# A new hand-written order with batch 0's chain at its head, and output blocks stored as one transfer each, in a fused attention and token-mixing kernel

## The chip, the cores and the metric

The kernel runs on one core of a Trainium2 chip. Its time is the device time of one execution in microseconds (us), as a median over runs; beside that there is one profiled execution with its own time and a trace. Engines: PE is TensorE (PEld its weight loads), ACT is ScalarE, DVE is VectorE, POOL is GpSimd, SP is the sync engine, which here only issues transfers.

## What is computed

```python
def _attn_ref(q, k, v, p):              # q, k, v: (8, 8, 576, 64), p: (8, 8, 32, 64)
    scale = 1.0 / np.sqrt(q.shape[-1])
    def sm_attn(qq, kk, vv):
        s = scale * np.matmul(qq, kk.transpose(0, 1, 3, 2))
        a = np.exp(s - np.max(s, axis=-1, keepdims=True))
        return np.matmul(a / (np.sum(a, axis=-1, keepdims=True) + 1e-09), vv)
    p_packed = sm_attn(p, k, v)
    return sm_attn(q, p_packed, p_packed)

def _moe_ref(x, w_q, w_k, w_out):       # x: (8, 576, 512), w_q, w_k: (512, 64), w_out: (512, 512)
    wq, wk = x @ w_q, x @ w_k
    W_tok = np.einsum('bsd,btd->bst', wq, wk) / np.sqrt(w_q.shape[1])
    return np.maximum(np.einsum('bst,btd->bsd', W_tok, x), 0.0) @ w_out
```

The attention's output, with its 8 heads laid side by side, is the x of the second part. The output is (8, 576, 512) in float32.

## The kernel before

The work is cut into some 75 small operations per batch, each a Python function (`s0`, `pv`, `m0`, `o3` ...), for eight batches. Their order is written out by hand in the string `SCHEDULE`; a loop at the end of the kernel reads it from left to right and emits the instructions. Each engine works through its own part of the list strictly in order, so the list is at once the order on PE, ACT, DVE, POOL and SP.

An entry is `name@batch`, then what it needs: digits after a colon are the PSUM banks that a PE operation writes (five banks, 0 to 4, are dealt out this way; the other three hold the scores `s` and `e` in turn); a `c` or `f` after them says whether a 128-wide matmul is cut into two halves of 64 columns or left full; a trailing `s` or `v` is the engine that copies a result from PSUM to SBUF ("evicts" it), ACT or DVE; `g` is POOL (for `ml`), `p` and `s` behind `sc` are the queue that issues the store, SP or ACT.

The chain of one batch, in the names of the list:

- `LK`, `LQ`, `LV`: loads of k, q and v (576 KB each as bf16), issued by POOL, which also issues the loads of p and the weights (`LP`, `cw0` to `cw3`, `wo0`, `wo1`). Each goes to one of six buffers (`SLOTS`).
- `kt`, `ke` and `qt`, `qe`: k and q are transposed on PE in three parts and evicted. Batch 0 is different: its k comes in float32 by two SP transfers (`k_f`, line 171, halves A and B), is cast to bf16 (`cA0`, `cA1`, `cB0`, `cB1`), transposed (`kf0`, `kf1` from half A, `kf2`, `kf3` from half B) and evicted (`kfe0` to `kfe3`). `tp` and `lp` bring batch 0's p into the block matrix `pT_bd`, which `s` uses; `tr`, `lq0`, `lq1` bring that of the other batches.
- `s0`, `nm0` (or `nmA`, `nmB`), `ex0`, `ex1`, `rc1`: scores of p against k, their maximum (DVE), exponentials (ACT), reciprocals of the sums.
- `xt`, `xe`, `pv`, `pp`, `pt`, `pte`: the exponentials transposed and evicted, times v, scaled and masked, transposed.
- `e0`, `mx`, `sb`, `x`, `sm`, `rr`, `ml`: scores of q against the 32 packed rows, and their softmax (DVE for `mx`, `sb`, `sm`, `rr`, ACT for `x`, POOL or DVE for `ml`).
- `at`, `ae`, `pq`, `wk`, `wq`, `g`, `y`, `m0`, `m1`, `m2` with their evictions (`wke`, `wkx`, `wqe`, `ge`, `ye`, `r00` ... `r2`): the token mixing in a reordered form; `wq`, evicted by `wqe` to the tile `wqT`, holds one column per token.
- `o0` to `o4`, `oe0` to `oe4`: the projection with `w_out` in four blocks of 128 tokens and a fifth that two batches share, evicted to `o_sb0`, `o_sb1` (two blocks each) and `ox`.
- `st0`, `st1`, `st2` store `o_sb0`, `o_sb1`, `ox` from SP. For the last batch `sc0` to `sc3` store one block each, from SP or ACT.

The 576 tokens of a batch are laid out as 64 rows `sp` of 9 tokens `j`. Tokens of column group `j2` (0 or 1) lie in partitions 64\*j2 to 64\*j2+63 of `o_sb`, which is why each store is two transfers:

```python
for j2 in range(2):
    nc.sync.dma_start(ov[:, 4 * j2 + 2 * i:4 * j2 + 2 * i + 2, :], S_[b][f"o_sb{i}"][64 * j2:64 * j2 + 64])
```

`wm` at the head of the list runs matmuls on the identity whose result nobody reads (24 pairs of 64x128 with 128 columns).

Of the kernel before, what the change touches and what calls it, by code (L numbers as in the profile page):

```python
# [7 lines left out]


SCHEDULE = """  # L10
    wm@24:3 LQ@0 LV@0 LP@0 LK@1 LK@2 cB1@0s cA0@0s kf3@0:3 cw1@0 tp@0:1 kfe3@0s cw3@0 lp@0v
# [6 lines left out]
    pqe@0s xt1@1:1c qe0@1s ml0@0v xt0@1:3c at1@0:2c rc1@1 xe1@1v xe0@1s s0@2 qe1@1v at0@0:0c
    ae1@0s nm0@2 pv@1:43 ae0@0s LQ@3 ex1@2 wk@0:0c pp0@1 pp1@1 wq@0:1 wke@0s wkx@0 ex0@2
    pt@1:4c g@0:2 pte@1v wqe@0s rc1@2 e0@1:f ge@0v LK@5 y@0:3 xt0@2:0c mx0@1 ye@0s kt1@3:4  # L20
    xe0@2s pq@1:2 LQ@4 m0@0:31 pqe@1s xt1@2:0c r01@0s sb0@1 kt0@3:2 r00@0s LV@4 kt2@3:1
    ke0@3s o1@0:3c ke2@3v x0@1 ke1@3v m1@0:21 oe1@0v o0@0:4c r10@0s sm0@1 r11@0s qt2@2:2
    s0@3 xe1@2s oe0@0s qt1@2:1 rr0@1 nm0@3 o2@0:0c qe2@2s ml1@1g qt0@2:3 ml2@1g oe2@0v
    qe0@2s pv@2:24 ml0@1g qe1@2v ex0@3 at1@1:0c LK@6 pp1@2 at0@1:3c pp0@2 ae1@1s o3@0:1c
    LQ@5 ae0@1v ex1@3 pt@2:3c wk@1:0c pte@2s LK@7 wq@1:4 wke@1s wkx@1 rc1@3 pq@2:2 wqe@1s
    g@1:3 e0@2:f pqe@2s ge@1v oe3@0s y@1:4 xt0@3:0c mx0@2 ye@1s st1@0 m0@1:31 LQ@6 xt1@3:4c
    r01@1s kt1@4:2 xe1@3v st0@0 r00@1s kt0@4:1 xe0@3v ke1@4s sb0@2 pv@3:34 ke0@4s kt2@4:0
    pp0@3 x0@2 o1@1:2c LV@5 pp1@3 ke2@4v qt0@3:3 sm0@2 oe1@1s m2@1:0c s0@4 qe0@3s qt1@3:1
    r2@1s pt@3:2c rr0@2 o0@1:4c nm0@4 pte@3s ml2@2g ml0@2g qt2@3:3 oe0@1s o4@1:2c qe2@3v
    ex1@4 ml1@2g qe1@3v at0@2:3c kt2@5:0 ex0@4 ae0@2v kt0@5:1 LQ@7 at1@2:3c oe4@1s ke0@5v  # L30
    e0@3:c ke2@5s ae1@2v m1@1:12 mx0@3 wk@2:4c r11@1s xt0@4:3f r10@1s xt1@4:2f rc1@4 wke@2s
    wkx@2 pq@3:0 kt1@5:1 xe1@4s sb0@3 o3@1:4c pqe@3s ke1@5s qt1@4:0 oe3@1v xe0@4s s0@5
    qe1@4v x0@3 wq@2:2 nm0@5 g@2:1 qt2@4:4 ge@2s wqe@2s pv@4:13 sm0@3 ex0@5 ex1@5 o2@1:2c
    pp0@4 pp1@4 y@2:1 qt0@4:0 qe2@4v oe2@1s pt@4:3c qe0@4v ye@2s kt2@6:4 pte@4s rr0@3
    m0@2:12 ke2@6v m1@2:30 r01@2s ml1@3g e0@4:c r10@2v r00@2s xt0@5:2f rc1@5 r11@2s mx0@4
    ml2@3g kt0@6:4 ml0@3g xe0@5s pq@4:0 kt1@6:3 o3@2:1c pqe@4s ke1@6v ke0@6s LV@6 sb0@4
    at1@3:0c LV@7 o1@2:4c ae1@3s oe3@2v at0@3:3c x0@4 kt0@7:2 ae0@3v o0@2:0c ke0@7v oe1@2s
    sm0@4 kt1@7:2 oe0@2s kt2@7:4 s0@6 ke2@7s ke1@7v wq@3:3 qt2@5:2 wqe@3s qt0@6:4 qe2@5v
    qt1@5:0 qe0@6s wk@3:3c rr0@4 nm0@6 xt1@5:1f ml2@4g qe1@5s o2@2:2f ml0@4g xe1@5s wkx@3
    qt1@6:0 ex0@6 oe2@2v ml1@4g pv@5:41 wke@3v ex1@6 st1@2 qe1@6v g@3:2 pp1@5 at1@4:3f pp0@5  # L40
    ge@3s st1@1 at0@4:0f ae1@4s qt2@6:2 ae0@4v xt0@6:1c rc1@6 qe2@6s xt1@6:4c st0@1 xe0@6v
    s0@7 xe1@6v y@3:1 pt@5:3c nm0@7 ye@3s qt2@7:2 st0@2 pte@5s qt0@7:4 qe2@7s qt0@5:0
    wk@4:3c qe0@7v ex0@7 pv@6:21 wkx@4 qe0@5v wke@4s ex1@7 m1@3:34 pp0@6 qt1@7:0 r11@3s
    pp1@6 e0@5:c r10@3s qe1@7v m2@3:4f mx0@5 xt0@7:1f r2@3s xt1@7:0f o2@3:3f xe0@7s rc1@7
    xe1@7s sb0@5 o4@3:4f oe2@3s g@4:1 pt@6:3f ge@4v x0@5 wq@4:0 pte@6v pq@5:2 oe4@3v y@4:1
    o3@3:3c pqe@5s sm0@5 wqe@4s e0@6:c ye@4s oe3@3s m0@4:40 rr0@5 pv@7:21 st1@3 r01@4s mx0@6
    ml0@5g r00@4s m0@3:30 o1@4:4c r01@3s ml1@5g sb0@6 r00@3s o0@4:0c oe1@4s ml2@5g pp1@7
    x0@6 at1@5:4c pp0@7 at0@5:3c o1@3:1c ae1@5v oe0@4s sm0@6 o0@3:4c ae0@5s oe1@3s pq@6:3
    wk@5:2c oe0@3s rr0@6 pt@7:0f ml1@6g wke@5s wkx@5 st0@3 m1@4:41 pte@7s pqe@6v g@5:2
    r11@4s r10@4v e0@7:f ml2@6g ge@5s st2@1 ml0@6g pq@7:2 wq@5:4 mx0@7 pqe@7s at1@6:0c  # L50
    wqe@5s y@5:2 at0@6:3c o2@4:1c ae0@6s ae1@6v ye@5s sb0@7 wk@6:4c oe2@4s m0@5:02 wke@6s
    o3@4:3f r00@5s wkx@6 r01@5v x0@7 g@6:1 oe3@4v m1@5:04 o0@5:2c ge@6s sm0@7 r10@5s st1@4
# [17 lines left out]
def kernel(  # L70
# [60 lines left out]
    def halves(m):  # L131
        return (slice(0, P),) if m == "f" else (slice(0, 64), slice(64, P))

    def bank(k, shape, dtype, name):
        return psK.tile(shape, dtype, tag=f"k{k}", name=name)

    def evict(on, dst, src, func=COPY, scale=1.0):
        if on == "s":
            nc.scalar.activation(dst, src, func, scale=scale)  # L139
        elif func == RELU:  # L140
            nc.vector.tensor_scalar(dst, src, 0.0, None, op0=MAX)
        elif scale != 1.0:
            nc.vector.tensor_scalar(dst, src, scale, None, op0=MULT)
        else:
            nc.vector.tensor_copy(dst, src)  # L145
# [515 lines left out]

    def store_block(c, b, on):
        eng = nc.scalar if on == "s" else nc.sync
        ov = out[b].rearrange("(sp j) d -> sp j d", j=NJ)
        for j2 in range(2):
            eng.dma_start(ov[:, 4 * j2 + c, :], S_[b][f"o_sb{c // 2}"][64 * j2:64 * j2 + 64, c % 2])
# [62 lines left out]
```

## Time and profile before

| | |
|---|---|
| three runs | 132.22, 133.68, 132.2 us; median 132.22 us |
| the profiled execution | 131.66 us |
| its span, first to last instruction | 129.6 us |
| mean granted clock of PE | 0.934 of full speed |
| busy PE / DVE / ACT / POOL | 108.7 / 93.2 / 95.3 / 41.5 us |
| loads, issued by POOL | 14.49 MB, 66.7% of 16 DMA engines' span |
| stores and the first loads, issued by SP | 10.16 MB, 26.4% |

How to read the lines shown below: a group or a piece is named by engine, source line and `out<-in` with the program's tile names; x12 is a count; what stands in brackets is the engine's idle time just before and what ended it. In stretches (`a:b`) stand the elapsed time, the busy time of each engine with its instruction count, the granted clock, the DMA share and GB/s. Matmuls are pipelined, so busy times of neighbouring groups overlap a little.

### The profile page before, as it was taken

How to read it: one execution, taken by the hardware profiler on the slowest of the kernel's cores; microseconds unless marked ns; L12 is line 12 of the kernel's file. 1: busy time of each engine (PE TensorE's matmuls, PEld its weight loads, DVE VectorE, ACT ScalarE, POOL GpSimd, SP SyncE). 2: the span in 40 equal slices, each digit the busy share in tenths (PEclk: the TensorE clock that was granted, in tenths of full speed). 3: DMA queues.
4: the chain of work that ended last, by engine and by line, in shares of the span. 5: the costliest groups of instructions: out<-in, count | busy, mean ns of one | idle time of the engine just before them, and what ended most of it. 6: DMA issues, size and time to landing. Idle time of an engine off the chain costs nothing.

```text
span 129.6 us, 4472 instructions
## 1 busy us (share of the span) xinstructions
PE 108.7 (84%) x1940; PEld 78.7 (61%) x1944; DVE 93.2 (72%) x158; ACT 95.3 (74%) x187; POOL 41.5 (32%) x61
## 2 busy tenths in 40 slices
...
PEclk9995558967999999999999999999999999999995
...
GB/s 47 358 199 210 210 193 200 211 204 205 208 207 209 206 211 207 275 293 210 206 209 207 199 206 142 260 295 106 0 167 28 215 24 259 229 224 212 284 196 122
DMA packets 18275, 25.45 MB, mean 196 GB/s; under 512 B 2512, under 2 KB 14800, under 8 KB 18256
## 3 DMA queue, kind: packets, MB, share of 16 engines
q0 software_dynamic: 13920, 14.49, 66.7%
q1 hardware_dynamic: 4016, 10.16, 26.4%
q10 hardware_dynamic: 320, 0.52, 1.7%
...
## 4 chain that ended last, share of the span: by engine, by line
PE 49%; DVE 21%; ACT 16%; DMA 4%; issue 3%; ACTq 1%; SPq 1%; DVEq 0%
PE o_ps L640 15%; PE tp_h L272 8%; PE pv L347 4%; DVE nmax L303 4%; DVE mx L430 4%; DMA k_f<-in_k_dram 4%; DVE e L433 4%; PE s L294 3%; ACT e1T L312 3%; PE e_ps L413 3%; DVE rs L444 2%; ACT o_sb L139 2%; ACT kT L139 2%; PE m_ps L603 2%; ACT e L440 2%
## 5 line engine op out<-in xcount | busy, mean ns | idle before, releaser
L468 POOL TENSOR_TENSOR a<-e,rr 128x512 bf16<-128x512 f32 (+1 forms) x21 | 16.9, 828 | 52.7 <-DVE rr L447 27.8
L640 PE MATMUL o_ps<-w_out,reluT 128*64 128x512 bf16 (+1 forms) x216 | 31.7, 380 | 0.4 <-DVE wkx L543 0.2
L640 PEld LDWEIGHTS <-reluT 128*64 128x64 bf16 (+1 forms) x220 | 13.3, 108 | 10.2 <-issue 1.4
L139 ACT ACTIVATE reluT<-m_ps 128x512 bf16<-128x512 f32 x27 | 14.7, 601 | 1.7 <-PE m_ps L603 1.5
L139 ACT ACTIVATE o_sb<-o_ps 128x512 f32<-128x512 f32 (+1 forms) x24 | 13.6, 588 | 2.5 <-PE o_ps L640 2.3
L312 ACT ACTIVATE e1T<-s,nmax 128x576 bf16<-128x576 f32 x16 | 11.8, 740 | 4.5 <-DVE nmax L303 4.5
L272 PE MATMUL tp_h<-ident,q_sb 128*64 128x128 bf16 x288 | 13.1, 242 | 0.0
L272 PEld LDWEIGHTS <-q_sb 128*64 128x64 bf16 x288 | 11.5, 126 | 2.3 <-issue 0.9
L303 DVE TENSOR_REDUCE nmax<-s 128x2 f32<-128x1152 f32 (+1 forms) x9 | 10.7, 1200 | 2.9 <-PE s L294 2.9
L139 ACT ACTIVATE kT<-tp_h 128x768 bf16<-128x768 bf16 (+2 forms) x14 | 10.5, 780 | 2.3 <-PE tp_h L232 1.3
L430 DVE TENSOR_REDUCE mx<-e_ps 128x36 f32<-128x1152 f32 (+2 forms) x9 | 10.9, 1216 | 1.5 <-PE e_ps L402 1.0
L272 PE MATMUL tp_h<-ident,k_sb 128*64 128x128 bf16 x252 | 10.3, 224 | 1.1 <-ACT kT L139 0.9
L444 DVE TENSOR_REDUCE rs<-e 128x36 f32<-128x1152 f32 (+2 forms) x9 | 10.9, 1214 | 0.3 <-ACT e L440 0.2
L433 DVE TENSOR_TENSOR e<-e_ps,mx 128x1152 f32<-128x1152 f32 (+2 forms) x9 | 10.9, 1218 | 0.2
L347 PE MATMUL pv<-v_sb,e 64*128 64x256 bf16 x144 | 10.5, 287 | 0.2 <-DVE e L145 0.2
L440 ACT ACTIVATE e<-e 128x1152 f32<-128x1152 f32 (+2 forms) x9 | 9.6, 1067 | 0.9 <-DVE e L433 0.9
L272 PEld LDWEIGHTS <-k_sb 128*64 128x64 bf16 x252 | 8.6, 112 | 2.3 <-issue 1.5
L139 ACT ACTIVATE qT<-tp_h 128x768 bf16<-128x768 bf16 x11 | 8.7, 820 | 0.7 <-PE tp_h L272 0.7
L145 DVE COPY o_sb<-o_ps 128x512 f32<-128x512 f32 x9 | 6.1, 683 | 3.9 <-DMA out_dram<-o_sb 2.6
L355 DVE SCALAR_TENSOR_TENSOR pp<-pv,rrec,mask 128x256 bf16<-128x256 f32 x16 | 7.0, 479 | 2.4 <-PE pv L347 2.3
L294 PE MATMUL s<-kT,pT_bd 128*64 128x64 bf16 (+3 forms) x64 | 6.3, 322 | 2.8 <-ACT kT L139 2.8
L347 PEld LDWEIGHTS <-e 64*128 64x128 bf16 x144 | 7.1, 99 | 2.1 <-DVE e L145 0.6
...
## 6 DMA issues: line engine op xcount, KB each, us to landing
out_dram<-o_sb SPq DMA_DIRECT2D x28, 256.0 KB, 3.8
q_sb<-in_q_dram POOLq DMA_DIRECT2D x8, 576.0 KB, 17.5
v_sb<-in_v_dram POOLq DMA_DIRECT2D x8, 576.0 KB, 14.3
k_sb<-in_k_dram POOLq DMA_DIRECT2D x7, 576.0 KB, 15.3
k_f<-in_k_dram SPq DMA_DIRECT2D x2, 576.0 KB, 4.7
out_dram<-ox SPq DMA_DIRECT2D x8, 128.0 KB, 3.3
w_out<-in_moe_w_out_dram POOLq DMA_DIRECT2D x2, 256.0 KB, 11.4
out_dram<-o_sb ACTq DMA_DIRECT2D x4, 128.0 KB, 2.4
```

The lines of the kernel that those rows point to most:

```text
L139: nc.scalar.activation(dst, src, func, scale=scale)
L272: nc.tensor.transpose(tp[64 * g2:64 * g2 + 64, 2 * gp:2 * gp + 2, jj, :], S_[b][src][:, gp + 2 * g2, order[3 * t + jj]], ident,)
L294: nc.tensor.matmul(ps[64 * gp:64 * gp + 64, S * h2 + c0:S * h2 + c1], pT_bd[:, b, 2 * gp + h2].rearrange("d g l -> d (g l)"), S_[b]["kT"][ ...
L303: nc.vector.tensor_reduce(tile("nmax", [P, 2], fp32, b)[:, r], S_[b]["s1"][:, r], axis=AX, op=MAX, negate=True)
L312: nc.scalar.activation(tile("e1T", [P, NJ, 2, 64], bf16, b)[:, :, h2], S_[b]["s1"][:, h2].rearrange("r (j s) -> r j s", j=NJ), EXP, bias=S ...
L347: nc.tensor.matmul(ps[h2], S_[b]["e1"][r, j, :], S_[b]["v_sb"][r, :, j, :].rearrange("s (g gp) d -> s gp g d", gp=2), start=(j == 0), stop ...
L430: nc.vector.tensor_reduce(tile("mx", [P, NU, 1], fp32, b)[:, r], S_[b]["e"][:, r], axis=AX, op=MAX)
L433: nc.vector.tensor_tensor(tile("e2", [P, NU, L], fp32, b)[:, r], S_[b]["e"][:, r], S_[b]["mx"][:, r].to_broadcast((P, nu, L)), op=SUB,)
L440: nc.scalar.activation(e, e, EXP, scale=scale)
L444: nc.vector.tensor_reduce(tile("rs", [P, NU, 1], fp32, b)[:, r], src[:, r], axis=AX, op=ADD)
L468: (nc.gpsimd if on == "g" else nc.vector).tensor_tensor(tile("a2", [P, NU, L], bf16, b)[:, r], S_[b]["e2"][:, r], S_[b]["rr"][:, r].to_bro ...
L640: nc.tensor.matmul(ps[r], src[:, i, o:o + P][:, r], w_out[:, i, :], start=(i == 0), stop=(i == 3),)
```

## The change

The list is reordered from end to end (600 entries in both, the same operations but for `wm`): of the engine letters 43 evictions change from ACT to DVE and 35 from DVE to ACT, and `ml0` and `ml2` of batch 0 go from DVE to POOL. Batch 0's head now begins with `tp`, then a smaller `wm` (5 pairs, 512 columns each), then the casts and transposes of half A ahead of those of half B. In the last batch `sc2` is issued by ACT and `sc0`, `sc1`, `sc3` by SP; before, it was `sc0`, `sc3` by ACT and `sc1`, `sc2` by SP.

`wqe` writes the columns of `wqT` interleaved, so that partition 2\*sp + j2 of an output block holds what was in partition 64\*j2 + sp. The 128 partitions of a block then follow the order of the rows in the output, and `st0`, `st1` and each `sc` become one transfer from 128 partitions where there were two from 64. `st2` keeps its two.

```diff
@@ SCHEDULE
-    wm@24:3 LQ@0 LV@0 LP@0 LK@1 LK@2 cB1@0s cA0@0s kf3@0:3 cw1@0 tp@0:1 kfe3@0s cw3@0 lp@0v
-    cB0@0s cw0@0 cA1@0v kf2@0:4 kf1@0:0 kfe2@0v kf0@0:1 kfe0@0s kfe1@0s s0@0 nmA@0 nmB@0
-    ex0@0 qt0@0:2 LQ@1 qt2@0:0 ex1@0 qt1@0:1 qe0@0s xt0@0:3c xt1@0:4c xe0@0v qe2@0s xe1@0v
-    rc1@0 qe1@0s pv@0:34 cw2@0 pp1@0 tr@0:20 pp0@0 LV@1 pt@0:1c lq0@0v pte@0s lq1@0s e0@0:c
-    mxB@0 kt1@1:2 LK@3 kt0@1:0 mxA@0 kt2@1:4 sbB@0 ke2@1s sbA@0 xB@0 ke1@1s smB@0 kt2@2:4
-    wo1@0 kt1@2:1 ke0@1s rrB@0 wo0@0 ml1@0v ke2@2s s0@1 LQ@2 ke1@2v xA@0 nm0@1 LV@2 kt0@2:1
-    ke0@2v ex0@1 smA@0 qt2@1:2 LV@3 ex1@1 pq@0:3 qt0@1:0 ml2@0v rrA@0 qt1@1:4 qe2@1v LK@4
...
-    ae0@7s wk@7:4c st0@5 oe4@5v m0@6:01 wke@7s wkx@7 m1@6:23 r01@6s r00@6v g@7:4 st2@3
-    r11@6s wq@7:1 r10@6s o0@6:0c wqe@7v st2@5 ge@7s y@7:3 o1@6:2c ye@7s oe0@6s m1@7:13
-    m2@7:4f r11@7s o2@6:0f r2@7v oe1@6s r10@7v o3@6:3f oe2@6s st0@6 o4@7:2f oe3@6s st1@6
-    m0@7:30 oe4a@7v oe4b@7s o2@7:1f r00@7s r01@7s st2@7 o3@7:4f oe2b@7s oe2a@7s o1@7:0f
-    sc2@7p oe3@7s sc3@7s o0@7:3f oe1@7v sc1@7p oe0@7s sc0@7s
+    tp@0:0 wm@5:1 LQ@0 LV@0 cA0@0s cA1@0v LP@0 lp@0v LK@1 kf1@0:0 LK@2 cB0@0v cB1@0s kf0@0:4
+    kfe1@0s kf3@0:1 cw1@0 kfe0@0v kf2@0:2 kfe3@0s cw3@0 kfe2@0v s0@0 cw0@0 nmB@0 nmA@0
+    qt2@0:2 ex1@0 cw2@0 qt1@0:0 qt0@0:1 qe1@0v ex0@0 qe0@0v qe2@0s xt1@0:4c xt0@0:3c xe1@0s
+    xe0@0v rc1@0 pv@0:10 LQ@1 tr@0:32 pp0@0 LV@1 pp1@0 pt@0:0c lq0@0v pte@0s lq1@0s e0@0:c
+    mxB@0 kt2@1:4 LK@3 kt0@1:3 mxA@0 ke2@1s kt1@1:0 sbA@0 ke1@1s sbB@0 xA@0 ke0@1v xB@0
+    kt0@2:0 smA@0 wo1@0 kt2@2:3 s0@1 smB@0 wo0@0 ke2@2s kt1@2:4 LQ@2 rrA@0 rrB@0 pq@0:3
+    ke1@2s nm0@1 ml2@0g LV@2 ml1@0v ml0@0g ex0@1 ke0@2v at1@0:4c ex1@1 LK@4 qt0@1:2 ae1@0v
...
+    oe2@5v ml0@7g ye@6v m2@5:0c oe3@5s at1@7:2c r2@5v m0@6:31 ae1@7s st1@5 at0@7:4f r00@6v
+    o4@5:0f r01@6s st1@4 ae0@7v st0@5 m1@6:21 oe4@5v wq@7:3 r11@6s wk@7:4c st2@5 r10@6s
+    o0@6:0f wke@7s wkx@7 wqe@7s g@7:1 oe0@6s o1@6:4f ge@7s y@7:1 o3@6:3c ye@7v oe1@6v
+    m2@7:2c m1@7:10 r2@7s st0@6 o2@6:4f r10@7v r11@7s oe3@6s m0@7:20 oe2@6s o3@7:1f r00@7v
+    r01@7s st1@6 o4@7:2f oe3@7v o1@7:3f sc3@7p oe4a@7v oe4b@7s st2@7 o0@7:1f oe1@7s o2@7:3f
+    sc1@7p oe0@7s sc0@7p oe2a@7v oe2b@7s sc2@7s
...
@@ -558,7 +558,10 @@
 
     @op
     def wqe(b, on):
-        evict(on, tile("wqT", [P, 512], bf16, b), S_[b]["wq_ps"])
+
+
+        dst = tile("wqT", [P, 512], bf16, b).rearrange("r (c s j) -> r c j s", c=4, j=2)
+        evict(on, dst, S_[b]["wq_ps"].rearrange("r (c j s) -> r c j s", c=4, j=2))
 
     @op
     def g(b, ks):
@@ -647,23 +650,23 @@
         r = slice(0, D) if half is None else slice(D // 2 * half, D // 2 * half + D // 2)
         evict(on, dst[:, r], S_[b]["o", c][:, r])
 
+    def rows_of(b):
+        return out[b].rearrange("(sp r) d -> sp r d", r=NJ)[:, 0:8].rearrange("sp (j c) d -> sp j c d", c=4)
+
     def store(i, b):
         if i == 2:
             for e in range(2):
                 ov = out[b - 1 + e].rearrange("(sp j) d -> sp j d", j=NJ)
                 nc.sync.dma_start(ov[:, 8, :], S_[b]["ox"][64 * e:64 * e + 64])
             return
-        ov = out[b].rearrange("(sp j) d -> sp j d", j=NJ)
-        for j2 in range(2):
-            nc.sync.dma_start(
-                ov[:, 4 * j2 + 2 * i:4 * j2 + 2 * i + 2, :], S_[b][f"o_sb{i}"][64 * j2:64 * j2 + 64],
-            )
+        nc.sync.dma_start(
+            rows_of(b)[:, :, 2 * i:2 * i + 2].rearrange("sp j c d -> sp j (c d)"),
+            S_[b][f"o_sb{i}"].rearrange("p c d -> p (c d)"),
+        )
 
     def store_block(c, b, on):
         eng = nc.scalar if on == "s" else nc.sync
-        ov = out[b].rearrange("(sp j) d -> sp j d", j=NJ)
-        for j2 in range(2):
-            eng.dma_start(ov[:, 4 * j2 + c, :], S_[b][f"o_sb{c // 2}"][64 * j2:64 * j2 + 64, c % 2])
+        eng.dma_start(rows_of(b)[:, :, c], S_[b][f"o_sb{c // 2}"][:, c % 2])
 
     for c in range(4):
         ops[f"sc{c}"] = lambda b, on, c=c: store_block(c, b, on)
@@ -679,12 +682,11 @@
 
     @op
     def wm(n, ks):
-        ps = bank(ks[0], [P, 128], fp32, "warm")
+        ps = bank(ks[0], [P, 512], fp32, "warm")
+        moving = ident.unsqueeze(1).to_broadcast((P, 4, P))
         for _ in range(n):
-            for g2 in range(2):
-                nc.tensor.matmul(
-                    ps[64 * g2:64 * g2 + 64], ident[:, 64 * g2:64 * g2 + 64], ident, start=True, stop=True,
-                )
+            for r in halves("c"):
+                nc.tensor.matmul(ps[r], ident[:, r], moving, start=True, stop=True)
 
     for item in SCHEDULE.split():
         name, rest = item.split("@")
```

More of the change, by code (lines that the diff above doesn't have):

```diff
@@ L17 @@
-    ke0@2v ex0@1 smA@0 qt2@1:2 LV@3 ex1@1 pq@0:3 qt0@1:0 ml2@0v rrA@0 qt1@1:4 qe2@1v LK@4
[L18 to L52, printed above, removed]
@@ new lines @@
+    kt0@2:0 smA@0 wo1@0 kt2@2:3 s0@1 smB@0 wo0@0 ke2@2s kt1@2:4 LQ@2 rrA@0 rrB@0 pq@0:3
+    ke1@2s nm0@1 ml2@0g LV@2 ml1@0v ml0@0g ex0@1 ke0@2v at1@0:4c ex1@1 LK@4 qt0@1:2 ae1@0v
+    qt1@1:0 pqe@0s rc1@1 at0@0:1c LV@3 qe0@1v qe1@1s xt0@1:4c xt1@1:3c ae0@0v s0@2 xe1@1v
+    xe0@1v qt2@1:0 wk@0:3c nm0@2 qe2@1s pv@1:14 LQ@3 wke@0s wkx@0 ex0@2 wq@0:0 pp0@1 pp1@1
+    ex1@2 g@0:2 pt@1:1f ge@0v wqe@0v y@0:3 pte@1s xt0@2:4c ye@0s e0@1:c xe0@2s LK@5 pq@1:2
+    mx0@1 m0@0:30 pqe@1s m1@0:41 r00@0s r01@0s kt1@3:3 sb0@1 r10@0s o1@0:0c r11@0s kt2@3:2
@@ new lines @@
+    ke1@3v x0@1 o0@0:1c oe1@0v kt0@3:3 ke2@3s sm0@1 xt1@2:0c qt1@2:4 ke0@3s o2@0:2c oe0@0s
+    rr0@1 xe1@2v qt0@2:3 oe2@0s ml0@1g qe1@2v s0@3 qe0@2v qt2@2:4 ml1@1g nm0@3 at0@1:3c
+    qe2@2s pv@2:10 ml2@1g ae0@1v LQ@4 ex1@3 at1@1:2c rc1@2 pp0@2 o3@0:4c LV@4 ae1@1s pp1@2
+    pt@2:3c LK@6 ex0@3 wq@1:2 pte@2v wk@1:1c LQ@5 wqe@1s xt1@3:3f xt0@3:0f wke@1s xe1@3v
+    e0@2:f xe0@3s wkx@1 rc1@3 kt0@4:1 oe3@0s mx0@2 kt1@4:2 ke0@4s g@1:0 st1@0 pq@2:4 kt2@4:3
+    ge@1s st0@0 ke1@4v pqe@2s y@1:1 sb0@2 ye@1s m0@1:41 pv@3:02 r00@1s ke2@4v x0@2 m2@1:4c
```

28 lines of the change are left out of this document (26 added, 2 removed).

## The prediction

> **What bounds the kernel now.** I read the page's busy table and its slices first. All times are microseconds unless marked ns; a slice is 3.24 us, its digit the clock granted to TensorE in tenths.
>
> ```profile
> span 129.6 us, 4472 instructions
> PE 108.7 (84%) x1940; PEld 78.7 (61%) x1944; DVE 93.2 (72%) x158; ACT 95.3 (74%) x187; POOL 41.5 (32%) x61
> ...
> PEclk9995558967999999999999999999999999999995
> ```
>
> TensorE is busiest, but its clock is at half in much of the first 32 us, so I looked at the kernel by stretches (elapsed time, then busy time of PE, PEld, DVE, ACT, POOL, then the clock).
>
> ```profile
> 30.50:122.62 92.12, 89.36 (x1603) 62.79 (x1602) 77.17 (x126) 79.52 (x159) 25.07 (x32) 1.00 0.92 196
> 122.62:129.60 6.98, 0.00 (x0) 0.00 (x0) 0.00 (x0) 0.60 (x1) 0.00 (x0) 0.75 0.63 172
> ```
>
> From 30.5 on TensorE is dense: 2.76 of 92.12 idle. Behind its last matmul stand 6.98 without it. So three things can move the end: when the dense middle starts, how much idle time the new order leaves in it, and the 6.98. The chain of waits (start, length, what) shows the first.
>
> ```profile
> 1.24 0.46 SPq L171
> 1.74 5.19 DMA k_f<-in_k_dram
> 6.95 1.26 ACT k_sb L139 x2
> 8.21 0.48 ACT kT L139
> 8.69 0.63 ACT k_sb L139
> 9.37 1.18 PE tp_h L232 x28
> 10.57 1.20 ACT kT L139 x2
> 11.81 1.19 PE s L294 x7
> 13.02 1.43 DVE nmax L303 x2
> 14.55 1.56 ACT e1T L312 x4
> 16.15 0.76 PE tp_x L330 x8
> 16.93 0.50 DVE e L145
> 17.48 2.43 PE pv L347 x18
> ```
>
> Nothing is computed for batch 0 until the second half of its k has landed at 6.93 (1.74 + 5.19); then casts, transposes, scores (`s`), softmax and `pv` follow in line. The timeline shows the end.
>
> ```profile
> 121.66 1.18 ACTq L666 DMA_DIRECT2D out_dram<-o_sb  x2
> 121.79 0.69 DVE L145 COPY o_sb<-o_ps 128x512 f32<-128x512 f32 x1 [2.60 <-DMA out_dram<-o_sb]
> 122.94 0.60 ACT L139 ACTIVATE o_sb<-o_ps 128x512 f32<-128x512 f32 x1 [1.31 <-PE o_ps L640]
> 123.57 1.12 ACTq L666 DMA_DIRECT2D out_dram<-o_sb  x2
> 124.25 2.65 SPq L666 DMA_DIRECT2D out_dram<-o_sb  x4
> ```
>
> The last block is in SBUF at 123.54, but SP begins four of the last eight half stores only at 124.25 and needs 2.65 to issue them.
>
> **Part 1, the front.** Before, the first casts are `cB1` and `cA0`, both on ACT: the half of k that lands first waits for the other. After, `cA0` (ACT) runs beside `cA1` and `lp` (DVE), and TensorE's order is `kf1 kf0 kf3 kf2`.
>
> ```profile
> k_f<-in_k_dram SPq DMA_DIRECT2D x1, 576.0 KB, 4.2
> L145 DVE CAST k_sb<-k_f x1: 516/516/516, 9.1 to 9.1; 128x512 bf16<-128x512 f32 x1
> L143 DVE TENSOR_SCALAR pT_bd<-tp_p x2: 283/288/294, 8.4 to 8.7; 64x128 bf16<-64x128 f32 x2
> 12.73 2.18 PE L272 MATMUL tp_h<-ident,q_sb 128*64 128x128 bf16 x36
> ```
>
> The first of the two k_f issues takes 4.2 to landing (last column), so half A is there at 1.24 + 4.2 = 5.45. `cA1` (0.52) ends at 5.97, the two instructions of `lp` (0.29 each) at 6.5. `kf1` writes the bank that `lp` reads, so it starts at 6.55. A transpose takes 2.18/36 = 61 ns at half clock (the last row lies in a half-clock slice), 1.18/28 = 42 ns at a mostly full one. At half clock, argued below, `kf1` (8 of them) and `kf0` (10) end at 7.65. Half B lands at 6.93, its casts (ACT 0.63, DVE about 0.65) end at 7.6, so `kf3` and `kf2` end at 8.73. `kfe1` and `kfe3` on ACT (1.20 for two) end at 8.8; `kfe2` on DVE (0.5) at 9.3. `s` starts at 9.35 instead of 11.81, 2.46 earlier. From there I use the chain's durations: `s` to 10.55, `nmax` to 12.0, the exponentials to 13.65. Then 0.4 is given back, because `xt1` now stands ahead of `xt0`, whose copy `pv` needs first: 18 transposes at about 65 ns to 14.85, `xe0` 0.50, `pv` at 15.45 instead of 17.48. The steps behind `pv` keep their order. **Front: -2.0.**
>
> The moved pieces around it: `qe1` and `qe0` go from ACT to DVE (about 0.55 each, by the 0.50 of the chain's `DVE e` for a sixth less) and run in DVE's gap between `nmax` (12.0) and `xe0` (14.85); without that gap they would cost 1.1. `tp` now stands ahead of the warm-up and waits for p_f, which SP issues before k_f and which is a ninth of half A in size; TensorE's next work for the chain is `kf1` at 6.55, so this costs nothing. On ACT `qe2` stands ahead of `xe1`; both end by 15.1, before `pv`.
>
> The clock: the new warm-up has ten matmuls of 512 columns for forty-eight of 128.
>
> ```profile
> 106.85 1.73 PE o_ps L640 x16
> 6.60:10.00 3.40, 1.30 (x31) 1.02 (x33) 1.21 (x4) 2.37 (x4) 2.74 (x6) 1.00 1.18 202
> 13.40:16.80 3.40, 2.47 (x44) 2.04 (x40) 1.05 (x2) 2.25 (x6) 0.80 (x2) 0.50 1.22 210
> 16.80:20.25 3.45, 3.29 (x35) 2.09 (x33) 1.22 (x4) 1.40 (x3) 0.74 (x1) 0.50 1.42 195
> ```
>
> Two 64-wide matmuls of 512 columns run as a pair in 1.73/8 = 0.22, so the new warm-up lasts about 1.1, and the stretch before 6.6 holds about 1.4 busy of 3.4. After a stretch with 1.30 busy the clock went to half, after 2.47 it stayed there, after 3.29 it came back. So I take half clock from 6.6 (0.4 on the start of `s`, counted above) until `pv` has run. The new front has 2.8 busy in the 3.4 after 6.6, between 2.47 and 3.29: if that brings the clock back, `pv` takes 1.1 and `s` about half, and the front is -4; if the clock comes back one stretch later than before, about 1 is lost. I keep -2.0, range -1 to -4.
>
> [...]
>
> The loads: POOL's ninth load waits for its first to land, the tenth for the second, and so on, so the rows in which POOL waited date the landings of q, v and batch 1's k.
>
> ```profile
> 9.98 0.75 POOL L149 DMA_DIRECT2D q_sb<-in_q_dram  x1 [0.66 <-DMA q_sb<-in_q_dram]
> 12.84 0.61 POOL L253 DMA_DIRECT2D wqk<-in_moe_w_k_dram  x1 [2.11 <-DMA v_sb<-in_v_dram]
> 18.31 0.74 POOL L149 DMA_DIRECT2D k_sb<-in_k_dram  x1 [3.50 <-DMA k_sb<-in_k_dram]
> ```
>
> q is there by 9.98 and needed at 10.55, v by 12.84 and needed at 15.45, batch 1's k by 18.31 and needed about 20.5. `cw2` passes `LQ@1` on POOL, so `LQ@1` is issued at 12.84 instead of 9.98, still behind batch 1's k in a queue that is never empty (the DMA share, last column but one of the stretches, is 1.18 and more): no change. Two more `ml` of batch 0 move to POOL, ahead of `LV@2` and `LK@4`. They delay these issues by a few us; the eight loads in flight cover that, and without the cover `pv@2` would wait as long.
>
> **Part 2, the middle.** The matmul work is the same. Counted in the two lists, 43 evictions go from ACT to DVE and 35 the other way.
>
> ```profile
> L141 DVE TENSOR_SCALAR reluT<-m_ps 128x512 bf16<-128x512 f32 x5 | 3.4, 683 | 0.0
> L143 DVE TENSOR_SCALAR pT_bd<-tp_r x4: 375/381/395, 20.7 to 21.7; 64x224 bf16<-64x224 bf16 x4
> ```
>
> Net eight at about 0.66 put 5.3 on DVE and bring it to 98, still below TensorE. What the reshuffle does to the 2.76 of idle time can't be read from the trace; it can gain at most that. I take 0, with -1.5 to +2. The wqT eviction now writes its columns interleaved. The nearest copy that writes in scattered pieces is `lq`, 224 elements in 381 ns against 128 in 288 in `lp`: 1 ns for each further element, no dearer than a plain copy. So 0, and 0.7 at most (a doubled write on the last batch's path).
>
> [...]
>
> **Part 3, the end.** Each store becomes one transfer from 128 partitions; the last eight half stores become four.
>
> ```profile
> SPq L666 <- DMA out_dram<-o_sb: 2.6, 1, 2.6
> out_dram<-o_sb SPq DMA_DIRECT2D x4, 128.0 KB, 2.5
> out_dram<-o_sb SPq DMA_DIRECT2D x1, 256.0 KB, 3.0
> ```
>
> SP's wait of 2.6 is for another store. In the program the transfers of SP and ACT share eight completion counters in turn, and the one that `sc2` needs is held by `sc3`, which ACT issued at 121.66. With one transfer per store the last eight reach back to `st0@6`, and the wait goes. Late next is the last block itself: at TensorE's end T, two DVE half copies (0.85 for both, a whole one being 0.69), the issue at T+0.9 taking 0.56, and then what followed the last issue before, 129.6 - 126.9 = 2.7, plus 0.5 for 256 KB against 128 KB (3.0 against 2.5): T+4.7, and T+5.0 with the store of `sc0` on its way at the same time. Bounds: T+4.2 without the two surcharges, T+5.8 if it takes as long as two in line. Against T+6.98 that is **end: -2.0**, range -1.2 to -2.8.
>
> **Sum.** The profiled execution took 131.66, 2.06 beyond its span: 131.66 - 2.0 + 0 - 2.0 = 127.7. The median of the three runs is 132.22, by which it is 128.2. I say 127.9, between the two.
>
> **Rivals.** *Clock back early*: front -4 instead of -2, 125.9. For it: 2.8 busy of 3.4; against: 2.47 did not do. *Front gain absorbed*: the middle starts no earlier, because DVE or a load sets it, and only the end gains: 129.9. For it: the load queue is full from 6.6 on; against: 0.5 to 2.6 of margin in the three load rows. *End unchanged*: the single store is as slow as two, and ACT's queue holds `sc2` up: 129.5. *Slower*: in the reshuffled middle an eviction that TensorE waits for stands once per batch behind one of DVE's softmax passes (1.43 over a batch's scores). Price up to 8 x 1.43 = 11.4; from 0.5 per batch it eats the gain of 4, from 0.83 it is over 2% slower; at 1.0 it is 135.9. For it: eight more evictions on DVE; against: DVE idles 15 of the 92 us.
>
> **Chances.** Forecast 0.53, clock early 0.15, absorbed 0.14, end unchanged 0.07, slower 0.11. The range, 125.6 to 131.0, leaves out the slower case and the tails. Faster by over 2% (below 129.6; 2% is about what a measurement of this kernel can tell from no change) are nearly all of the first two and under half of the next two: 0.75. Slower by over 2% 0.10, within 2% 0.15.
>
> **What would show it.** Right: the first k cast near 5.5, `s` near 9.4, `pv` near 15.5, the dense middle from about 28.5, the last matmul's end near 120.6, no wait of SP on a store at the end, and about 5 from T to the end. Wrong: a clock still at half past 20, idle time of TensorE in the middle well above 2.8, or a last store that lands over 4 after its issue.

## The result and the profile after

The changed kernel takes 127.81 us in the median (126.32 to 128.14), the kernel before 132.21 beside it: a ratio of 0.962, 95% interval 0.952 to 0.972. The execution shown below took 127.78, with a span of 125.6. Below, a ratio is always to the kernel before run beside the kernel in question. Medians are over all runs, while ratios leave out those in a slower state: two of four in e2, for which no ratio is given, and one of four in e5, e9 and e10, whose medians without it are 124.76, 125.95 and 126.33.

First the head of the page after, as it was shown of before (span, busy times, the clock in slices of 3.14 us).

```profile
span 125.6 us, 4311 instructions
PE 108.3 (86%) x1870; PEld 77.0 (61%) x1874; DVE 98.0 (78%) x164; ACT 91.8 (73%) x179; POOL 43.3 (34%) x63
...
PEclk9999959996899999999999999999999999999998
```

Then the same two stretches (elapsed, then busy time of PE, PEld, DVE, ACT, POOL, then clock, DMA share, GB/s), cut where TensorE's last matmul ends.

```profile
30.50:121.08 90.58, 88.71 (x1541) 62.24 (x1541) 77.57 (x123) 76.32 (x150) 24.60 (x32) 0.99 0.88 202
121.08:125.60 4.52, 0.00 (x1) 0.00 (x0) 0.42 (x1) 0.38 (x1) 0.00 (x0) 0.89 0.61 205
```

TensorE ends at 121.08 instead of 122.62, and 4.52 follow instead of 6.98. So 2.46 of the 4.0 by which the span is shorter stand at the end, and only 1.54 come from all that lies before. That is too little for the front, as the chain of waits of after shows (start, length, what).

```profile
9.25 0.99 PE s L294 x5
...
14.87 1.67 PE pv L347 x15
...
32.83 1.09 PE pv L347 x18
```

Batch 0's `pv` starts at 14.87 instead of 17.48, 2.6 earlier. The next rows are from the timeline of before: the scores of batch 0's memory (`e_ps`), a multiply of batch 0's softmax on DVE (`ml1`, L468), and batch 1's `pv`, which after starts at 32.76 by the timeline (32.83 in the chain).

```profile
21.70 0.25 PE L402 MATMUL e_ps<-ppT,qT 128*64 128x64 bf16 x4 [0.48 <-ACT ppT L139]
26.69 0.69 DVE L468 TENSOR_TENSOR a<-e,rr 128x512 bf16<-128x512 f32 x1
32.79 1.16 PE L347 MATMUL pv<-v_sb,e 64*128 64x256 bf16 x18
```

So the whole gain of the front is gone one stage later. It is still there at `e_ps`, 2.62 earlier than before; from `e_ps` to batch 1's `pv` the changed kernel then takes 13.68 where the kernel before took 11.09. What happens in between is in the timeline of after, here `e_ps`, DVE's `nmax` and `ml1`, POOL beside them, and TensorE's `at1` (L497).

```profile
19.08 0.25 PE L402 MATMUL e_ps<-ppT,qT 128*64 128x64 bf16 x4 [0.47 <-ACT ppT L139]
24.83 1.29 DVE L303 TENSOR_REDUCE nmax<-s 128x2 f32<-128x1152 f32 x1
26.04 1.94 DVE L468 TENSOR_TENSOR a<-e,rr 128x512 bf16<-128x512 f32 x1
25.53 0.81 POOL L149 DMA_DIRECT2D v_sb<-in_v_dram  x1
26.36 1.06 POOL L468 TENSOR_TENSOR a<-e,rr 128x512 bf16<-128x512 f32 x1
28.03 0.41 PE L497 MATMUL tp_a<-ident,a 128*64 128x128 bf16 x8 [2.97 <-ACT pqk L139]
```

`ml1` takes 1.94 where the same instruction took 0.69 before, while POOL issues a load and runs `ml0`, a multiply that the change moved there (1.93 or 1.94 also in e2, e7 and e10, which have the same order there). TensorE stands 2.97 before `at1`, which reads what `ml1` writes; the releaser named in the bracket, `pqk` on ACT, also ends at 27.98, but in e6, below, `at1` starts at 25.91, and there the bracket names `a` on DVE. Behind that idle stretch the clock falls, as the stretches of after show:

```profile
23.60:27.00 3.40, 1.39 (x34) 0.96 (x28) 3.40 (x6) 2.46 (x5) 1.86 (x3) 1.00 1.20 203
27.00:30.40 3.40, 2.37 (x62) 2.37 (x64) 2.95 (x6) 1.79 (x4) 3.13 (x5) 0.80 1.23 206
30.40:33.80 3.40, 3.40 (x58) 2.60 (x54) 2.45 (x4) 1.46 (x3) 0.25 (x1) 0.70 1.23 210
```

**The theories.** M, read off these rows: the front's gain is eaten in stage 2 (the steps between batch 0's `pv` and batch 1's), the rest gains a little, the end 2.5. R is the prediction: front -2.0 carried through, middle 0, end -2.0. Both give the measured sum, so the experiments had to take the parts one by one.

### The profile page after: what moved, and what is told of

It is laid out like the page before. It is cut to its first block, busy times and chain, and to the rows that moved or that the text cites. A ratio compares the mean times of both kernels' runs of the same rounds, so it can differ in the third digit from the quotient of the medians.

```text
span 125.6 us, 4311 instructions
## 1 busy us (share of the span) xinstructions
PE 108.3 (86%) x1870; PEld 77.0 (61%) x1874; DVE 98.0 (78%) x164; ACT 91.8 (73%) x179; POOL 43.3 (34%) x63
## 4 chain that ended last, share of the span: by engine, by line
PE 75%; DVE 9%; ACT 6%; DMA 5%; issue 1%; SPq 0%; ACTq 0%
PE o_ps L643 23%; PE tp_h L272 11%; PE pv L347 7%; PE tp_x L330 4%; PE s L294 4%; PE e_ps L413 3%; PE m_ps L606 3%; DMA k_f<-in_k_dram 3%; PE wq_ps L553 3%; ACT e1T L312 2%; PE wk_ps L529 2%; DVE nmax L303 2%; PE tp_h L232 2%; DMA out_dram<-ox 2%; PE tp_a L488 2%; PE tp_a L497 2%
## 5 line engine op out<-in xcount | busy, mean ns | idle before, releaser
L468 POOL TENSOR_TENSOR a<-e,rr 128x512 bf16<-128x512 f32 (+1 forms) x23 | 18.4, 822 | 56.0 <-DVE rr L447 28.8
L643 PE MATMUL o_ps<-w_out,reluT 128*64 128x512 bf16 (+1 forms) x205 | 32.2, 380 | 0.2
L643 PEld LDWEIGHTS <-reluT 128*64 128x64 bf16 (+1 forms) x208 | 13.4, 107 | 9.7 <-issue 1.5
L139 ACT ACTIVATE reluT<-m_ps 128x512 bf16<-128x512 f32 x25 | 14.0, 598 | 2.6 <-PE m_ps L606 2.4
L139 ACT ACTIVATE o_sb<-o_ps 128x512 f32<-128x512 f32 (+1 forms) x22 | 12.6, 593 | 2.8 <-PE o_ps L643 1.9
L272 PEld LDWEIGHTS <-q_sb 128*64 128x64 bf16 x288 | 10.9, 120 | 1.7 <-issue 0.4
L139 ACT ACTIVATE kT<-tp_h 128x768 bf16<-128x768 bf16 (+1 forms) x13 | 9.9, 776 | 1.0 <-PE tp_h L272 0.8
L139 ACT ACTIVATE qT<-tp_h 128x768 bf16<-128x768 bf16 x9 | 7.3, 816 | 4.3 <-PE tp_h L272 4.3
L347 PE MATMUL pv<-v_sb,e 64*128 64x256 bf16 x144 | 9.8, 279 | 0.6 <-DVE e L145 0.6
L145 DVE COPY o_sb<-o_ps 128x512 f32<-128x512 f32 (+1 forms) x11 | 7.2, 652 | 2.9 <-PE o_ps L643 2.9
L145 DVE COPY qT<-tp_h 128x768 bf16<-128x768 bf16 x15 | 7.9, 548 | 0.0
## 6 DMA issues: line engine op xcount, KB each, us to landing
k_sb<-in_k_dram POOLq DMA_DIRECT2D x7, 576.0 KB, 13.4
```

What stands on the lines that cost most here:

```text
L272: nc.tensor.transpose(tp[64 * g2:64 * g2 + 64, 2 * gp:2 * gp + 2, jj, :], S_[b][src][:, gp + 2 * g2, order[3 * t + jj]], ident,)
L347: nc.tensor.matmul(ps[h2], S_[b]["e1"][r, j, :], S_[b]["v_sb"][r, :, j, :].rearrange("s (g gp) d -> s gp g d", gp=2), start=(j == 0), stop ...
L468: (nc.gpsimd if on == "g" else nc.vector).tensor_tensor(tile("a2", [P, NU, L], bf16, b)[:, r], S_[b]["e2"][:, r], S_[b]["rr"][:, r].to_bro ...
L643: nc.tensor.matmul(ps[r], src[:, i, o:o + P][:, r], w_out[:, i, :], start=(i == 0), stop=(i == 3),)
```

## The experiments

**The parts one by one.** e1 is the kernel before with the change's `wqe`, `rows_of`, `store` and `store_block`; e2 is the other half, the new SCHEDULE and `wm` with the old stores. e3 and e5 are the changed kernel with parts of SCHEDULE put back (the lists agree in which steps have been done at the cuts; items numbered from 0):

```diff
 e3: -SCHEDULE = new
     +SCHEDULE = new[:51] + old[51:]
 e5: -SCHEDULE = new
     +SCHEDULE = new[:51] + old[51:118] + new[118:]
```

> The order and the warm-up of before, with only the stores as one transfer each and the interleaved columns. Theory M, read off the two traces: the end shrinks by about 2.5 (no SP wait on a store, 4.5 to 4.8 from TensorE's last matmul to the end) and the rest stays, so 129.7 against 132.2. Theory R, the prediction on record: the end shrinks by 2.0, 130.2. If the completion counter was not what SP waited for, nothing moves: 132.2.

Measured: 129.08 (127.81 to 129.69), ratio 0.976, interval 0.969 to 0.983. The time behind TensorE's last matmul is 4.15 in its profile, and SP no longer waits for a store. That is the mechanism of M and R, with a sum 0.6 below M's 129.7.

```profile
123.15:127.30 4.15, 0.00 (x0) 0.00 (x0) 0.00 (x0) 0.60 (x1) 0.00 (x0) 1.00 0.62 232
```

> The new order and the new warm-up, with the stores as two half transfers each and the old eviction of wqT. M: the front's gain is mostly eaten in stage 2 and the middle gains about 1.5 by TensorE's end, so 130.3 if the old end of 6.98 stays, and down to 129.5 if the new order of the last stores avoids part of SP's wait. R: front -2.0 carried, 130.2. The two agree here; what tells them apart is the time of batch 1's pv: 32.8 (M) or 30.8 (R).

Measured: 130.73 and 128.97 in the two runs that can be compared, too few for a ratio. In the trace batch 1's `pv` starts at 32.03, nearer to M's time; the 0.73 that it is ahead of the changed kernel is already there at `e_ps` (18.30), and from there it takes 13.73, as in the changed kernel (13.68). That is M's reading: the loss is in stage 2. The order alone doesn't mend the end: with half stores SP still waits 2.5 for one (from the waits: who waited, total, times, longest), and 8.05 follow the last matmul.

```profile
SPq L666 <- DMA out_dram<-o_sb: 2.5, 1, 2.5
120.65:128.70 8.05, 0.00 (x0) 0.00 (x0) 0.42 (x1) 0.38 (x1) 0.00 (x0) 0.66 0.59 139
```

> The changed kernel with the old order behind batch 0's pv (the first 51 items new, the rest as before). If the front's gain is eaten by the new order of stage 2, the old rest keeps it: pv of batch 1 near 30.2 and 127.2 or less in all. If it is eaten whatever follows (a load or the clock), batch 1's pv stays near 32.8 and the time is 129.7, which is the gain of the end alone.

Measured: 125.40 (125.24 to 126.83), ratio 0.952, interval 0.945 to 0.958: by the medians 2.4 faster than the changed kernel, and 3.7 faster than e1, which differs from it by the front alone. Its timeline:

```profile
14.88 1.16 PE L347 MATMUL pv<-v_sb,e 64*128 64x256 bf16 x18 [0.59 <-DVE e L145]
17.79 0.25 PE L402 MATMUL e_ps<-ppT,qT 128*64 128x64 bf16 x4 [0.47 <-ACT ppT L139]
28.98 1.16 PE L347 MATMUL pv<-v_sb,e 64*128 64x256 bf16 x18
```

Batch 1's `pv` starts at 28.98, which is 3.8 earlier than in both kernels. Of the 3.8 against the changed kernel, 1.3 stand ahead of `e_ps` (17.79 against 19.08), which both reach by the same instructions, and 2.5 behind it. The front's gain carries if the old order follows it. So neither a load nor the clock eats it whatever follows.

> The changed kernel with only stage 2 (the items between batch 0's pv and the batch 1 softmax and pv) in the old order, the front and the rest new. M, stage 2's order eats the front's gain: batch 1's pv about 2 earlier, 125.8. Rival, a load or the clock eats it: 127.8, as the changed kernel, and batch 1's pv near 32.8.

Measured: 124.81 (124.51 to 126.51), ratio 0.944, interval 0.939 to 0.949: stage 2's new order costs 3.0 of the changed kernel's time by the medians, 2.4 by the ratios. DVE's `ml1` is there 3.2 earlier and as short as before:

```profile
22.85 0.69 DVE L468 TENSOR_TENSOR a<-e,rr 128x512 bf16<-128x512 f32 x1
...
28.66 1.16 PE L347 MATMUL pv<-v_sb,e 64*128 64x256 bf16 x18
```

By medians the change then consists of: stores -2.9 (132.01, the kernel before beside these four, to 129.08), front -3.7 (to 125.40), the rest without stage 2 -0.6 (to 124.81), stage 2 +3.0 (to 127.81). By the ratios, of 132, it is -3.2, -3.2, -1.0 and +2.4. The gain of the rest isn't shown: the intervals of e3 and e5 overlap.

**What in stage 2 costs 3.0.** Three theories. P: the POOL multiply beside `ml1` makes it 1.94 long. D: DVE now does both halves of batch 0's softmax in turn, and `nmax` of batch 1, before `ml1`, so that it starts too late. Q: `at1` stands too early in TensorE's order and holds up transposes that are ready.

```diff
 e6: -... ml2@0g LV@2 ml1@0v ml0@0g ex0@1
     +... ml2@0g LV@2 ml1@0v ml0@0v ex0@1
 e7: -... at1@0:4c ex1@1 LK@4 qt0@1:2 ae1@0v qt1@1:0 pqe@0s
     +... ex1@1 LK@4 qt0@1:2 qt1@1:0 at1@0:4c ae1@0v pqe@0s
 e8: -sbA@0 ... sbB@0 xA@0 ... xB@0 ... smA@0 ... smB@0 ... rrA@0 rrB@0 ... nm0@1 ml2@0g LV@2 ml1@0v ml0@0g
     +sbB@0 sbA@0 ... xB@0 xA@0 ... smB@0 rrB@0 ml1@0v smA@0 ... rrA@0 ... nm0@1 ml2@0g LV@2 ml0@0g
```

> The changed kernel with one multiply of batch 0 (ml0) on DVE behind ml1 instead of on POOL beside it. Theory P, the POOL operation slows ml1 from 0.69 to 1.94: ml1 takes 0.69 again, at1 starts at 26.8 instead of 28.0, and about 1.2 is gained: 126.6. Theory D, ml1 starts 3.2 too late because DVE now does both halves of batch 0's softmax in turn: ml1 still starts at 26.0, so no more than the 1.2 of P comes back, and not the 3.0 that the old order of stage 2 gave. Theory Q, the position of at1 in TensorE's order alone: 127.8.

Measured: 124.83 (124.11 to 125.33), ratio 0.946, interval 0.941 to 0.950. P's step is right, its sum is too small: one letter brings back 3.0 by medians (2.2 by the ratios), not 1.2.

```profile
18.21 0.25 PE L402 MATMUL e_ps<-ppT,qT 128*64 128x64 bf16 x4 [0.48 <-ACT ppT L139]
25.18 1.27 DVE L468 TENSOR_TENSOR a<-e,rr 128x512 bf16<-128x512 f32 x2
25.91 0.41 PE L497 MATMUL tp_a<-ident,a 128*64 128x128 bf16 x8 [1.71 <-DVE a L468]
29.44 1.16 PE L347 MATMUL pv<-v_sb,e 64*128 64x256 bf16 x18
27.00:30.40 3.40, 3.40 (x90) 3.02 (x89) 3.38 (x8) 2.01 (x4) 0.74 (x1) 1.00 1.22 205
```

Two multiplies on DVE now take 1.27, less than one beside POOL's. POOL issues loads beside them all the while (24.66 to 26.96), so it is POOL's multiply that slows `ml1`, not the issue of a load. From the start of `e_ps` to `at1` it is 7.70 instead of 8.95 (25.91 - 18.21 against 28.03 - 19.08): P's 1.25. But from `at1` to batch 1's `pv` it is also less, 3.53 instead of 4.73, and the last row shows the clock at full where the changed kernel had 0.80 and then 0.70. That gave theory K: the other 1.2 is the clock, closed by the longer idle stretch.

> The changed kernel with at1 of batch 0 (and its eviction) moved behind qt0 and qt1 of batch 1 in TensorE's order. Theory Q, TensorE stands 2.97 before at1 while 24 transposes of 0.92 in all are ready behind it: batch 1's pv comes 0.9 earlier, 126.9. Theory D, what sets batch 1's pv is when ml1 is done, and the transposes only change places with it: within 0.4 of 127.8.

Measured: 126.90 (126.36 to 127.87), ratio 0.961, interval 0.956 to 0.965. The median is Q's, but by the ratios it can't be told from the changed kernel (0.962), and the trace shows that Q's mechanism did not act:

```profile
27.07 0.85 PE L272 MATMUL tp_h<-ident,q_sb 128*64 128x128 bf16 x12 [2.08 <-DVE kT L145]
27.67 0.69 PE L497 MATMUL tp_a<-ident,a 128*64 128x128 bf16 x8
32.67 1.34 PE L347 MATMUL pv<-v_sb,e 64*128 64x256 bf16 x18
23.60:27.00 3.40, 0.56 (x14) 0.42 (x13) 3.40 (x3) 2.34 (x6) 3.27 (x5) 0.89 1.20 206
27.00:30.40 3.40, 3.10 (x52) 2.87 (x53) 1.44 (x5) 0.81 (x1) 1.22 (x2) 0.50 1.23 207
```

The second group of transposes waits 2.08 for a copy on DVE that stands behind `ml1` and frees the bank that they write, so they were not ready; TensorE does 0.56 in the 3.4 before 27.0, and the next 3.4 run at half clock. From `e_ps` (17.65) to batch 1's `pv` it takes 15.02, longer than the changed kernel's 13.68.

> The changed kernel with DVE and ACT doing the second half (B) of batch 0's softmax first and ml1 right behind it, ahead of the first half's sum and of batch 1's nmax; engines of all steps and TensorE's order as changed. Theory D: ml1 starts near 23.5 instead of 26.0, TensorE's wait before at1 goes, and most of the 3.0 comes back: 125.0 to 125.8. Theories P and Q: ml1's own length and at1's place are what cost, so no more than 1.2 comes back: 126.6 to 127.8.

Measured: 124.84 (123.86 to 125.70), ratio 0.946, interval 0.940 to 0.952: D's range, or a little better.

```profile
24.26 0.69 DVE L468 TENSOR_TENSOR a<-e,rr 128x512 bf16<-128x512 f32 x1
24.41 0.80 POOL L468 TENSOR_TENSOR a<-e,rr 128x128 bf16<-128x128 f32 x1 [1.34 <-DVE rr L447]
25.49 0.41 PE L497 MATMUL tp_a<-ident,a 128*64 128x128 bf16 x8 [0.53 <-ACT kT L139]
30.60 1.16 PE L347 MATMUL pv<-v_sb,e 64*128 64x256 bf16 x18
```

`ml1` starts 5.15 behind `e_ps` (19.11) instead of 6.96, runs clear of `ml0` and takes 0.69; the POOL row is `ml2`, a smaller multiply beside it. TensorE's wait before `at1` is 0.53, and no clock is lost in stage 2 (1.00 in every stretch from 20.25 to 33.8). This edit also takes `ml1` away from `ml0`, so it doesn't refute P: D and P are two ways to lose the same wait, and either edit alone brings the time back.

**Theory K by itself.** e10 leaves `ml1` as long as it is and only fills TensorE's idle stretch:

```diff
-... ke0@2v at1@0:4c ex1@1
+... ke0@2v wm@10:1 at1@0:4c ex1@1
```

> The changed kernel with twenty matmuls that compute nothing put on TensorE ahead of at1 of batch 0, where it stands idle for 2.97; ml1 still takes 1.94 beside the POOL multiply. Theory K: of the 3.0 that taking the multiply off POOL gained, 1.25 is the longer ml1, and the rest is TensorE's clock, which the longer idle stretch closes from 29.0 to 32.4. The fillers keep it open, at1 comes no earlier but batch 1's pv follows it by 3.5 instead of 4.7: 126.6. Without K (the whole 3.0 hangs on ml1's time): 127.8, or more if the fillers are in the way.

Measured: 126.68 (126.00 to 128.11), ratio 0.960, interval 0.952 to 0.968. The time alone, K's figure within 0.1, doesn't tell it from the changed kernel; the trace does.

```profile
28.18 0.41 PE L497 MATMUL tp_a<-ident,a 128*64 128x128 bf16 x8 [0.82 <-ACT pqk L139]
31.32 1.16 PE L347 MATMUL pv<-v_sb,e 64*128 64x256 bf16 x18
27.00:30.40 3.40, 2.58 (x74) 2.04 (x72) 3.25 (x7) 1.94 (x6) 2.80 (x4) 1.00 1.23 206
```

`at1` is no earlier (28.18 against 28.03), the clock stays at 1.00 where the changed kernel had 0.80, and `pv` follows after 3.14 instead of 4.73. That is one execution: two of the four runs had a mean clock of 0.963, no higher than the changed kernel's 0.963 to 0.977.

The traces side by side, from the start of `e_ps` to that of batch 1's `pv`. Up to `e_ps` the instructions are the same in all but the kernel before, yet its start differs by up to 1.6 from one execution to another, so only the last column can be compared.

| | `e_ps` | `pv` of batch 1 | between |
|---|---|---|---|
| before | 21.70 | 32.79 | 11.09 |
| after | 19.08 | 32.76 | 13.68 |
| e3, old order behind the front | 17.79 | 28.98 | 11.19 |
| e5, old stage 2 | 17.86 | 28.66 | 10.80 |
| e6, `ml0` on DVE | 18.21 | 29.44 | 11.23 |
| e7, `at1` later | 17.65 | 32.67 | 15.02 |
| e8, half B first | 19.11 | 30.60 | 11.49 |
| e10, fillers | 19.22 | 31.32 | 12.10 |

So in the traces stage 2's loss, 2.5 to 2.9, has two parts of about equal size: 1.25 for the slowed multiply, 1.2 to 1.6 for the clock.

**The warm-up.** e9 is e3 without the ten warm-up matmuls.

```diff
-tp@0:0 wm@5:1 LQ@0
+tp@0:0 LQ@0
```

> The new front on the old rest (125.4) with the ten warm-up matmuls left out. Theory W, the warm-up opens TensorE's clock and the denser chain behind it keeps it: without it the clock is at half from the first transposes on until the chain has been dense for a while, the 28 transposes and the scores take 1.5 to 2 longer, 127.2. Theory C, the chain alone, 2.5 us earlier and denser, opens the clock: 125.4. The prediction on record had the clock at half from 6.6 in any case, which is 2 or more above 125.4.

Measured: 125.99 (125.46 to 127.91), ratio 0.954, interval 0.950 to 0.957, against 0.952 for e3: theory C. In its trace batch 0's `pv` starts at 14.75, e3's at 14.88. The warm-up's new shape explains none of the gain; at most 0.6 by the medians hangs on having one.

**Versions on top.** e11 is e5, e12 is e6, each with fillers (`wm@`) in TensorE's waits and the last block copied whole; e13 is e12 with the last 37 items in the old order.

```diff
 e11: +wm@3:3 ahead of xt1@0, +wm@2:3 ahead of kt2@2, +wm@3:3 ahead of s0@1
 e12: ml0@0v, +wm@3:3 ahead of xt1@0, +wm@3:1 ahead of at1@0
 both: -oe2a@7v oe2b@7s
       +oe2@7s
 e13: e12's edits of the front and stage 2, then old[563:]
```

> New front, old stage 2, new rest (124.8) with fillers of the same kind in TensorE's waits: six ahead of batch 0's xt1, four and six in stage 2's waits; and the last block copied whole on ACT instead of in two halves. Theory K: the clock no longer falls back in the front, 0.6 on the average of the runs, and the whole copy ends 0.3 earlier: 123.9. Without K: 124.5, and the fillers may cost up to 0.5 where they stand in the way: 125.0.

> The changed kernel with ml0 of batch 0 on DVE (124.8), fillers ahead of batch 0's xt1 (six) and at1 (six), and the last block copied whole on ACT. K: 123.9, as the other. Without K: 124.5 to 125.0.

Measured: e11 124.46 (ratio 0.944, interval 0.937 to 0.950), e12 124.24 (0.942, 0.934 to 0.949). K's half of the expectation came: the clock of the four runs was 0.99 to 1.00 in both, against 0.981 to 0.995 in e5 and 0.965 to 0.983 in e6. In time, by the ratios, neither can be told from the kernel that it builds on (e5 0.944, e6 0.946), so what the fillers are worth isn't shown. The whole copy's half of the expectation did not come: 4.69 and 5.13 follow the last matmul instead of 4.52, with the last store landing in 2.8 and 3.3 instead of 2.5.

> The changed kernel with ml0 of batch 0 on DVE, six fillers ahead of batch 0's xt1 and six ahead of its at1, and the old order of the last 37 items, whose last block is one whole copy and one store on ACT (end 4.1 to 4.2 behind TensorE's last matmul in the two kernels that had this order, 4.5 in the changed one). If these three add up: 124.2 less 0.4 to 0.9 for the end, 123.6. If the end is given back in TensorE's order ahead of it: 124.2 to 124.6.

Measured: 123.85 (123.27 to 124.16) against 131.15 for the kernel before beside it, ratio 0.944, interval 0.940 to 0.948. 4.12 follow its last matmul, so in the trace the old order of the last items is worth what was expected of it; in the ratio e13 and e12 are the same, and both beat the changed kernel by about 2%.

## Why the prediction came out, and where its steps did not

The sum was right, 127.9 against 127.81, but not because each term was; that it came within 0.1 is luck. Against -2.0, 0 and -2.0 stand, by the medians, -3.7 for the front, +2.4 for the middle (stage 2 +3.0, the rest -0.6) and -2.9 for the end; the first and last errors, -1.7 and -0.9, cancel the middle's 2.4. By the ratios it is -3.2, +1.4 and -3.2, with errors of the same signs.

- **Front, casts to `pv`: right in kind, short in size.** The first cast was at 5.30 (5.45), `s` at 9.25 (9.35; one of its matmuls already at 8.45), `pv` at 14.87 (15.45), all in the places named. The term was -2.0 and measured -2.6 at `pv` in the changed kernel's trace.
- **Front, the clock: the step that failed.** "I take half clock from 6.6 until `pv` has run" held, by durations, up to the transposes of q (61 ns each) and was too dark behind them: the 18 transposes ahead of `pv`, priced at about 65 ns, took 38 each, which is 0.5 of the 0.58 by which `pv` came before its forecast.

```profile
10.14 2.06 PE L272 MATMUL tp_h<-ident,q_sb 128*64 128x128 bf16 x34
13.58 0.69 PE L330 MATMUL tp_x<-ident,e1T 128*64 128x128 bf16 x18 [1.38 <-ACT e1T L312]
```

The rival *clock back early*, put at -4, is what some executions show: `e_ps` starts 3.9 earlier than before in e3 (17.79 against 21.70), where `pv` took 1.16, and 2.6 earlier in the execution of the changed kernel, where it took 1.67, with the same instructions up to there. How often each happens isn't shown.
- **The warm-up** took 2.34, not 1.1, without effect on the time (e9). In e10 twenty of these matmuls take 2.35, so ten can run in 1.2; the clock column says 1.00 in both places (3.0 to 6.4 in the changed kernel, 23.6 to 27.0 in e10).
- **Middle, `ml` moved to POOL: the step that failed most.** Part 1 priced the two moved multiplies only by the loads queued behind them on POOL. What they cost was on DVE, 1.25 in `ml1`, and through it a clock dip (0.80, then 0.70) of 1.2 to 1.6. The range of the middle was -1.5 to +2; it came out at +2.4 by the medians, and at +1.4, inside the range, by the ratios. In e8 it was POOL's multiply that took longer: `ml2` 0.80 beside `ml1`, against 0.40 in e6, where no multiply ran on DVE at that time, and `ml1` kept its 0.69. Which of the two is held up doesn't follow from which starts first: `ml1` starts 0.32 ahead of `ml0` in the changed kernel, behind the start of POOL's issue of a load, and takes 1.94; it starts 0.15 ahead of `ml2` in e8. No run shows why.
- **The rival *absorbed*** had the right place and the wrong cause: no load set the start of the middle, and the gain was not hidden but spent. What the rival *slower* describes is shown once, as theory D: work that TensorE waits for stood behind DVE's softmax passes in batch 0.
- **End: right in mechanism.** SP waits only for copies now, 0.6 and 0.3:

```profile
SPq L669 <- DVE o_sb L145: 0.6, 1, 0.6
SPq L669 <- ACT o_sb L139: 0.3, 1, 0.3
out_dram<-o_sb SPq DMA_DIRECT2D x3, 256.0 KB, 2.4
```

The end was put at T+5.0 and measured T+4.52. The two half copies, one on DVE and one on ACT and not both on DVE as the prediction has it, and the issue ended at T+1.61, where its terms gave T+1.46. Too large were the terms behind the issue: 2.9 followed it and not 3.5 (2.7, 0.5 and 0.3), with 256 KB landing in 2.4 to 2.5 and not 3.0. e1 shows that the stores do it, e2 that the order without them makes the end longer, 8.05. That the wait was for a shared completion counter is argued from the program; no run changes the counter alone.
- **wqT's interleaved columns: put at 0, and not quite free.** In e1, which has them in the old order, the copy to `wqT` takes 0.75 on ACT where it took 0.60 before, and 0.74 on DVE where it took 0.69 (seven copies on ACT, by the median, and one on DVE). So the reading from `lq`'s copies on DVE doesn't carry over to ACT, and writing two bytes of every four was not free there. e1's total is lower all the same; what these copies cost it isn't shown.
- **Its own signs.** `s`, `pv` and SP's waits came as named. The dense middle from 28.5 did not: TensorE was busy 2.37 of the 3.4 up to 30.4, and the clock was down again between 27.0 and 33.8 (0.80, then 0.70). The last matmul ended at 121.08, not 120.6.
